# Moving a small PSUM copy from ScalarE to VectorE in a float32 Fourier transform and two-layer perceptron

## The chip, the cores and the metric

The kernel runs on one core of one Trainium2 chip. The metric is device time in microseconds, as the median of several runs. The kernel before takes 1793.97 us (median of 3 runs, 1788.93 to 1805.12).

Five engines run beside each other, each with its own queue of instructions that it works off in order: TensorE (PE in the profile; its weight loads are PEld), VectorE (DVE), ScalarE (ACT), GpSimd (POOL) and SyncE (SP, which here only issues transfers). They tell each other by semaphores what is done.

## The reference

For each of 8 batches of 3008 x 256 float32 numbers, the real part of the two-dimensional discrete Fourier transform is taken. Each of the 24064 rows of the result then goes through a perceptron with a squared ReLU:

```python
def _attn_ref(x) -> np.ndarray:
    X = np.fft.fft(x, axis=1)
    X = np.fft.fft(X, axis=2)
    return X.real.astype(np.float32)
...
def _moe_ref(x, w_in, w_out, s, b) -> np.ndarray:
    h = x @ w_in
    r = np.maximum(h, 0.0)
    g = s * (r * r) + b
    return (g @ w_out).astype(np.float32)
```

The weights are 256 x 2048 and 2048 x 256.

## The kernel before

**Transform along the sequence.** The symmetry of a real transform folds each batch into eighths on VectorE (`load`, lines 488 to 493). `transform(su, ph)` then makes the spectrum of batch `su` in two phases, `ph` 0 and 1. Each phase has four *pairs*. For a pair, TensorE makes eight small float32 matmuls of 96 columns (line 555) into one PSUM tile `ab` that holds two halves, `l[:, :, 0]` and `l[:, :, 1]`. `both` (lines 560 and 561) then takes the sum and the difference of the halves on VectorE, one half from PSUM and the other from an SBUF tile `t`. The helper `two` fills that `t`: it copies the second half out of PSUM (line 566). In phase 0 two of the four pairs call `two`, in phase 1 all four: 6 copies of 128 x 192 numbers in a batch, 48 in all. Further calls of `both` combine these into `x` and `o`, the spectrum in float32.

**Split into two reduced numbers.** `store` splits `o` into a high and a low float32r part: ScalarE casts it to `spec_h` (line 540), GpSimd subtracts to get `spec_l` (line 542).

**The perceptron.** The transform along the features is folded into the first weights at the start, so each of 3 blocks of a batch is 16 steps of `first_layer` and `second_layer`, 384 steps in all. A step's first layer is six matmuls of 502 columns into a PSUM tile `ab` (line 618), three additions on VectorE that make `h` (lines 620 to 622; the last one frees the PSUM tile), ReLU and square on ScalarE (623, 624), ScalarE's cast to `gh` (631) and GpSimd's subtraction to `gl` (634). The second layer is twelve matmuls of 502 columns into four accumulators `po` (line 651), which `finish` reads on VectorE at the end of a block (line 674).

**Buffers.** The PSUM tile `ab` has two buffers, used in turn by the pairs and by the first layers. So TensorE can start the next pair or first layer only when VectorE has read the last but one. `t` has two buffers, `x`, `o` and `lf` have one, `h`, `gh` and `gl` three.

**What sets the order.** Two strings of letters, `START` and `BATCH`, are the order in which the pieces of work are issued, and `_in_order` fixes this order on TensorE, VectorE, ScalarE and GpSimd. `L` is a first layer, `S` a second layer, `l` a piece of the next batch's folding, and `v` and `o` are pieces of the next batch's transform, phase 0 and 1. `START` holds the decoding of the weights, the transform of the first batch (`s`, `u`), all of the second's, and 57 first layers; `BATCH` is then issued in a loop, a *round* for each further batch: 48 first layers and 48 second layers of one batch with the transform of the next one between them. Six rounds have a transform in them. When a round begins, three first layers are ahead of their second layers.

The piece of code of a pair up to its `yield` issues the matmuls; what follows, the copy and the sums, comes with the next letter. In ScalarE's queue the copy stands behind the activations and casts of the first layers that were issued before it, and in VectorE's queue line 560 stands behind those layers' additions.

## Time and profile before

| | |
|---|---|
| runs | 1793.97 us, median of 3 (1788.93 to 1805.12) |
| profiled execution, its own time | 1792.28 us |
| its span, first to last instruction | 1790.2 us |
| TensorE busy | 1697.7 us, 95% |
| VectorE busy | 1281.8 us, 72% |
| ScalarE busy | 1258.8 us, 70% |
| GpSimd busy | 927.2 us, 52% |
| mean granted TensorE clock | 0.987 |
| copies of line 566 on ScalarE | 48, 14.4 us |

The start lasts until about 330 us, the six rounds with a transform from there to 1624 us, and the rest to 1790 us is the last batch's perceptron with no transform beside it. In a row of the timeline stand the start, the length, the engine, the line, the operation, output <- inputs with their shapes, how many, and in brackets how long the engine was idle before and for whom. A row of the waits has the engine with line, whom it waited for, microseconds in total, times, and the longest. Matmuls are pipelined: a matmul of 502 columns shows some 390 ns, while the next one starts 0.23 us after it.

### The profile page before, as it was taken

To read this page: it belongs to the slowest core of one execution; us is meant where nothing else is said; L and a number is where in the kernel's file an instruction comes from. 1 tells how busy PE (TensorE), PEld (TensorE's weight loads), DVE (VectorE), ACT (ScalarE), POOL (GpSimd) and SP (SyncE) were. 2 spreads that over 40 slices of the span, in tenths; PEclk is the share of its full clock that TensorE was granted. 3 is DMA by queue.
4 is the path that set the end of the run, shared out by engine and by line. 5 is a ranking of instruction groups with operands and counts; after the bars stand their busy time and mean duration, and the time that the engine had idled before them with its cause. 6 is when DMAs were issued, how large, how long until landed. Compare 5 with 4: busy or idle time off the path is not lost.

```text
span 1790.2 us, 21386 instructions
## 1 busy us (share of the span) xinstructions
PE 1697.7 (95%) x7526; PEld 1388.3 (78%) x7526; DVE 1281.8 (72%) x1957; ACT 1258.8 (70%) x1349; POOL 927.2 (52%) x562
## 2 busy tenths in 40 slices
PE   4899998999999999999999999999999999999999
PEld 3678777787787787887788777888778777788887
DVE  7888866796569766697567975679667896575554
ACT  2787776577677776776767666677776777677776
POOL 4555554454455554554545445554554554555554
PEclk9999999999999999999999999999999999999999
DMA  5321101110001100020000200002000110000000
GB/s 168 88 74 52 63 10 29 39 62 29 1 30 50 50 29 7 24 75 26 29 7 33 73 24 24 24 16 82 15 24 30 29 54 29 1 29 6 24 24 24
DMA packets 25313, 67.37 MB, mean 38 GB/s; under 512 B 4915, under 2 KB 9875, under 8 KB 25206
## 3 DMA queue, kind: packets, MB, share of 16 engines
q1 hardware_dynamic: 24934, 64.83, 11.4%
q0 software_dynamic: 272, 1.18, 0.3%
q8 instruction: 59, 0.97, 0.2%
q14 instruction: 48, 0.39, 0.1%
HBM read 41.27 MB, written 24.73 MB: 37 GB/s over the span
## 4 chain that ended last, share of the span: by engine, by line
PE 69%; DVE 17%; ACT 8%; issue 4%; DMA 1%; POOL 0%; SPq 0%; DVEq 0%; ACTq 0%; POOLq 0%
PE po L651 44%; PE ab L618 22%; DVE h L620 3%; DVE h L621 3%; ACT h L624 3%; ACT h L623 3%; DVE h L622 3%; PE ab L555 2%; ACT gh L631 2%; DVE xt L488 2%; DVE cs L493 1%; PE ab L319 1%; DVE o L674 1%; DVE xt L490 1%; DVE o L560 1%
## 5 line engine op out<-in xcount | busy, mean ns | idle before, releaser
L634 POOL TENSOR_TENSOR gl<-h,gh 128x1004 fp32r<-128x1004 f32 x373 | 811.7, 2176 | 758.2 <-ACT gh L631 482.4
L623 ACT ACTIVATE h<-h 128x1004 f32<-128x1004 f32 x384 | 400.1, 1042 | 386.3 <-DVE h L622 374.9
L620 DVE SCALAR_TENSOR_TENSOR h<-ebc,wny,ab 128x502 f32<-128x502 f32 x384 | 281.2, 732 | 299.1 <-PE ab L618 286.2
L651 PE MATMUL po<-gh,wo_h 128*128 128x502 f32 (+1 forms) x1536 | 487.0, 398 | 3.0 <-DVE o L674 3.0
L651 PE MATMUL po<-gh,wo_l 128*128 128x502 f32 (+1 forms) x1536 | 479.9, 394 | 0.0
L651 PE MATMUL po<-gl,wo_h 128*128 128x502 f32 (+1 forms) x1536 | 478.9, 393 | 0.6 <-POOL gl L634 0.6
L631 ACT CAST gh<-h 128x1004 fp32r<-128x1004 f32 x384 | 397.2, 1034 | 18.5 <-PE po L651 6.4
L624 ACT ACTIVATE h<-h 128x1004 f32<-128x1004 f32 x384 | 401.1, 1044 | 12.2
L618 PE MATMUL ab<-spec_h,wd_h 128*128 128x502 f32 x768 | 307.1, 400 | 47.2 <-DVE h L622 37.7
L651 PEld LDWEIGHTS po<-gl,wo_h 128*128 128x128 f32 x1536 | 293.5, 191 | 62.9 <-POOL gl L634 2.2
L651 PEld LDWEIGHTS po<-gh,wo_l 128*128 128x128 f32 x1536 | 293.2, 191 | 62.8
L651 PEld LDWEIGHTS po<-gh,wo_h 128*128 128x128 f32 x1536 | 290.3, 191 | 62.1 <-ACT gh L631 3.5
L618 PE MATMUL ab<-spec_l,wd_h 128*128 128x502 f32 x768 | 301.6, 393 | 0.3 <-POOL spec_l L542 0.3
L618 PE MATMUL ab<-spec_h,wd_l 128*128 128x502 f32 x768 | 300.5, 391 | 0.0
L622 DVE TENSOR_TENSOR h<-h,ab 128x502 f32<-128x502 f32 x384 | 260.4, 678 | 13.2
L621 DVE TENSOR_TENSOR h<-h,ab 128x502 f32<-128x502 f32 x384 | 260.2, 678 | 13.2
L618 PEld LDWEIGHTS ab<-spec_h,wd_h 128*128 128x128 f32 x768 | 146.6, 191 | 94.8 <-DVE h L622 52.9
L618 PEld LDWEIGHTS ab<-spec_h,wd_l 128*128 128x128 f32 x768 | 145.8, 190 | 29.4
L618 PEld LDWEIGHTS ab<-spec_l,wd_h 128*128 128x128 f32 x768 | 146.8, 191 | 27.5 <-POOL spec_l L542 0.6
L560 DVE TENSOR_TENSOR t<-ab,t 128x192 f32<-128x192 f32 x48 | 17.1, 356 | 139.6 <-ACT t L566 139.4
L542 POOL TENSOR_TENSOR spec_l<-o,spec_h 128x368 fp32r<-128x368 f32 (+3 forms) x80 | 62.0, 796 | 51.4 <-ACT spec_h L540 50.8
L540 ACT CAST spec_h<-o 128x368 fp32r<-128x368 f32 (+3 forms) x80 | 31.5, 441 | 70.9 <-DVE o L561 70.6
(91 smaller groups left out, 810.7 us busy)
## 6 DMA issues: line engine op xcount, KB each, us to landing
xt<-in_xq SPq DMA_DIRECT2D x64, 384.0 KB
out<-o SPq DMA_DIRECT2D x46, 502.0 KB
raw<-in_w_in SPq DMA_DIRECT2D x8, 512.0 KB
raw<-in_w_out SPq DMA_DIRECT2D x8, 512.0 KB
ebc<-e_dram SPq DMA_DIRECT2D x16, 251.0 KB
ebc<-e_dram SPq DMA_DIRECT2D x8, 126.0 KB
out<-o SPq DMA_DIRECT2D x4, 251.0 KB
ebc<-e_dram SPq DMA_DIRECT2D x8, 125.0 KB
```

The lines of the kernel that those rows point to most:

```text
L488: add(t[:, 0::2], t[:, 0::2], t[:, 1::2])
L542: nc.gpsimd.tensor_sub(lo, src, hi.bitcast(F32))
L555: nc.tensor.matmul(ps[:, kind, i], data[i][:, at], dft_sb[:, ph, kind, leaf + i])
L618: nc.tensor.matmul(ps[:, kind], w[:, kind, fj], m[:, kind], start=i == 0, stop=i == 2)
L620: nc.vector.scalar_tensor_tensor(h[:, 0], ebc, wny[:, j:j + 1], ps[:, 0], op0=ALU.mult, op1=ALU.add)
L621: sub(h[:, 1], h[:, 0], ps[:, 1])
L622: add(h[:, 0], h[:, 0], ps[:, 1])
L623: nc.scalar.activation(h, h, AF.Relu)
L624: nc.scalar.activation(h, h, AF.Square)
L631: nc.scalar.copy(gh[:, :, :NT], h)
L634: engine.tensor_sub(gl[:, :, :NT], h, gh[:, :, :NT].bitcast(F32))
L651: nc.tensor.matmul(po[2 * pm + dh][:, :n], l[:, j, dh * P:(dh + 1) * P], r[:, pm, :n], start=start and first, stop=stop and last,)
```

## The change

The copy of a pair's second half out of PSUM is made by VectorE in place of ScalarE:

```diff
         def two(t, l):
 
             second = t[:, :, :NL]
-            nc.scalar.copy(second, l[:, :, 1])
+            nc.vector.tensor_copy(second, l[:, :, 1])
             return l[:, :, 0], second
```

The order on TensorE and GpSimd is the same in both kernels. On ScalarE 48 instructions go, on VectorE 48 come.

First, ScalarE at the first copy of a round (`t` is the copy's SBUF tile, `ab` the pair's PSUM tile; `h` and `gh` belong to first layers):

```order
 L624 ACTIVATE h<-h 128x1004 [waits Activation_49]
 L631 CAST gh<-h 128x2x502 [waits PE_49,Activation_49]
-L566 COPY t<-ab 128x2x96
 L623 ACTIVATE h<-h 128x1004 [waits DVE_49,Pool_49]
 L624 ACTIVATE h<-h 128x1004 [waits Activation_49]
```

The copy stood behind a first layer's activations and its cast; what was behind it moves up by one.

Second, VectorE at the same place of the program, the first pair of phase 0 of a round:

```order
 L621 TENSOR_TENSOR h<-h,ab 128x502 [waits DVE_49]
 L622 TENSOR_TENSOR h<-h,ab 128x502 [waits DVE_49]
-L560 TENSOR_TENSOR t<-ab,t 128x2x4x24 [waits PE_49,Activation_49]
+L566 COPY t<-ab 128x2x96 [waits PE_49]
+L560 TENSOR_TENSOR t<-ab,t 128x2x4x24 [waits DVE_49]
 L561 TENSOR_TENSOR t<-ab,t 128x2x4x24
 L620 SCALAR_TENSOR_TENSOR h<-ebc,wny,ab 128x502 [waits PE_49,Pool_49]
```

The copy stands directly ahead of the sum that reads it, and the wait for ScalarE is replaced by one for the pair's matmuls.

Third, VectorE at the last pair of phase 0 of a round (`o` is the finished spectrum that `store` splits, `lf` the input of phase 1):

```order
 L622 TENSOR_TENSOR h<-h,ab 128x502 [waits DVE_49]
-L560 TENSOR_TENSOR t<-ab,t 128x2x96 [waits Activation_49]
-L561 TENSOR_TENSOR t<-ab,t 128x2x96
-L560 TENSOR_TENSOR o<-x,t 128x4x96 [waits DVE_49,Pool_49]
+L566 COPY t<-ab 128x2x96
+L560 TENSOR_TENSOR t<-ab,t 128x2x96 [waits DVE_49]
+L561 TENSOR_TENSOR t<-ab,t 128x2x96
+L560 TENSOR_TENSOR o<-x,t 128x4x96 [waits DVE_49,Activation_49,Pool_49]
 L561 TENSOR_TENSOR o<-x,t 128x4x96
 L349 SCALAR_TENSOR_TENSOR lf<-cs,turn_sb 96x256 x2
```

Here too the copy comes in ahead of the first sum. The sum into `o` now waits for ScalarE itself.

## The prediction

> **What bounds the kernel now.** I began with the page's span and busy shares.

> ```profile
> span 1790.2 us, 21386 instructions
> ...
> PE 1697.7 (95%) x7526; PEld 1388.3 (78%) x7526; DVE 1281.8 (72%) x1957; ACT 1258.8 (70%) x1349; POOL 927.2 (52%) x562
> ```

> TensorE is the bound. Nothing on another engine is worth time unless TensorE stands still behind it, or its clock does. So the next view was the waits, in the loop's stretch (330 to 1624 us).

> ```profile
> DVE t L560 <- ACT t L566: 117.4, 30, 4.7
> ...
> PE ab L618 <- DVE h L622: 32.1, 19, 3.4
> PE ab L555 <- DVE t L561: 13.8, 6, 2.3
> PE po L651 <- DVE o L674: 3.0, 4, 1.4
> ```

> (us in total, times, longest.) VectorE waits for 30 of the loop's 36 copies of line 566, 3.9 us on average. That is VectorE's idle time and by itself costs nothing. The other three rows are TensorE's waits in the loop, all for VectorE. The question is which of them hang on the copy. There are two such places in each of the six loop rounds.

> The first place is the first pair of a transform's first phase (rows picked from the timeline; start, length, and in brackets the idle time before):

> ```profile
> 619.17 1.03 PE L555 MATMUL ab<-dft_sb,cs 96*128 96x96 f32 x8
> 620.93 0.68 DVE L622 TENSOR_TENSOR h<-h,ab 128x502 f32<-128x502 f32 x1
> 625.51 0.31 ACT L566 COPY t<-ab 128x192 f32<-128x192 f32 x1
> 625.86 0.36 DVE L560 TENSOR_TENSOR t<-ab,t 128x192 f32<-128x192 f32 x1 [4.25 <-ACT t L566]
> 626.63 1.10 PE L555 MATMUL ab<-dft_sb,lf 96*128 96x96 f32 x8 [2.29 <-DVE t L561]
> ```

> The pair's matmuls end at 620.20 and VectorE is free at 621.61. But the copy stands in ScalarE's queue, behind the work of a first-layer step, until 625.51. VectorE cannot read the pair until 625.86, the PSUM buffer is not freed, and TensorE stands 2.29 us.

> The second place is the last pair of that phase (rows picked in the same way):

> ```profile
> 666.98 1.04 ACT L540 CAST spec_h<-o 128x380 fp32r<-128x380 f32 x2
> 671.26 2.16 POOL L634 TENSOR_TENSOR gl<-h,gh 128x1004 fp32r<-128x1004 f32 x1
> 672.21 0.68 DVE L622 TENSOR_TENSOR h<-h,ab 128x502 f32<-128x502 f32 x1
> 676.25 2.16 POOL L634 TENSOR_TENSOR gl<-h,gh 128x1004 fp32r<-128x1004 f32 x1 [2.83 <-ACT gh L631]
> 676.42 0.36 DVE L560 TENSOR_TENSOR t<-ab,t 128x192 f32<-128x192 f32 x1 [3.53 <-ACT t L566]
> 676.69 0.35 DVE L561 TENSOR_TENSOR t<-ab,t 128x192 f32<-128x192 f32 x1
> 677.14 1.68 DVE L560 TENSOR_TENSOR o<-x,t 128x384 f32<-128x384 f32 x1
> 678.42 0.38 PE L618 MATMUL ab<-spec_h,wd_l 128*128 128x502 f32 x1
> 681.47 0.68 DVE L622 TENSOR_TENSOR h<-h,ab 128x502 f32<-128x502 f32 x1
> 682.20 0.50 PE L618 MATMUL ab<-spec_h,wd_h 128*128 128x502 f32 x1 [3.40 <-DVE h L622]
> ```

> VectorE loses 3.53 us on the copy. The o of line 560 then starts beside GpSimd's line 634 and takes 1.68 us. So the h behind them is done at 682.15, and TensorE, which wants its buffer, stands 3.40 us.

> Last I looked at the clock, by stretches (us, busy PE, PEld, DVE, ACT, POOL with counts, granted clock): a round without and a round with half-rate, the six rounds together, the stretch before the loop, and three short ones of the round at 758: around its first place, and behind its second.

> ```profile
> 545.71:758.46 212.75, 205.48 (x929) 169.71 (x929) 157.17 (x239) 153.10 (x161) 112.20 (x59) 1.00 0.11 34
> 758.46:975.49 217.03, 209.87 (x930) 172.96 (x929) 157.23 (x239) 153.09 (x161) 112.29 (x59) 0.98 0.10 33
> sum 1292.84, PE 1246.45 PEld 1027.36 DVE 947.13 ACT 918.07 POOL 671.01; mean PE 207.74 PEld 171.23 DVE 157.85 ACT 153.01 POOL 111.84
> 198.00:331.48 133.48, 122.83 (x538) 100.22 (x538) 86.93 (x140) 87.68 (x97) 67.05 (x38) 0.96 0.09 27
> 837.70:841.10 3.40, 1.72 (x12) 1.64 (x13) 2.42 (x5) 0.88 (x2) 2.14 (x1) 1.00 0.01 2
> 841.10:844.50 3.40, 3.40 (x10) 2.71 (x9) 2.33 (x5) 2.39 (x3) 0.00 (x0) 0.50 0.00 0
> 895.70:902.50 6.80, 5.99 (x14) 4.81 (x15) 4.81 (x8) 5.10 (x5) 2.63 (x2) 0.50 0.00 0
> ```

> The stretch of 3.4 us in which the first place's wait leaves TensorE busy for only 1.72 us is followed by one of 3.4 us at half clock. Behind the second place it is 6.8 us. So a long wait can cost twice.

> **The change part by part.** *The copy leaves ScalarE.* 48 copies of 0.31 us leave its queue. At 70% busy it has room, so this alone is worth nothing on TensorE's path.

> *The copy joins VectorE's queue*, directly ahead of the first line 560 that reads it (the order of the instructions shows this).

> ```profile
> L566 ACT COPY t<-ab x48: 292/312/323, 19.2 to 1615.2; 128x192 f32<-128x192 f32 x48
> ...
> L560 DVE TENSOR_TENSOR t<-ab,t x48: 342/358/360, 24.9 to 1615.6; 128x192 f32<-128x192 f32 x48
> L560 DVE TENSOR_TENSOR o<-x,t x24: 557/1762/1802, 50.2 to 1616.2; 128x384 f32<-128x384 f32 x24
> ```

> (ns, shortest, median, longest.) No such copy is in the trace. Its bounds are ScalarE's 0.31 us and 0.36 us for VectorE's sum over the same PSUM half and one more operand; I take 0.35 us, nearer to the row of its own engine. What needs its result starts 0.10 us after its end, as the o above does (676.69 + 0.35, then 677.14). So a copy costs VectorE 0.45 us from its start to the start of t, 21.6 us in all. It cannot be below nothing, since an instruction is added there.

> GpSimd could make it dearer. The o sums, which read two operands from SBUF, go from 557 ns to 1802 beside GpSimd's work; the t sums, with one operand in SBUF, never leave 342 to 360. The copy reads PSUM only, so I go by the t row. If it were held up like an o, it would cost 1.2 us more, which place two below would feel as half a microsecond a round, 3 us in all. [...]

> *The wait moves from ScalarE to TensorE.* At the first place VectorE is free at 621.61 and the pair has been done since 620.20. Copy to 621.96, t from 622.06, its second sum from 622.33 to 622.68. Without the stall TensorE would ask for the buffer at 626.63 - 2.29 = 624.34, so 1.7 us of margin: the 2.29 us go.

> At the second place the copy starts at 672.89, t at 673.34, o at 674.06. GpSimd's line 634 has ended at 673.42 and its next one waits for ScalarE's cast until 676.25, so o runs in 0.56 us instead of 1.68. From o's start to the end of the last h sum it was 682.15 - 677.14 = 5.01 us; less 1.12 us that is 3.89, so 677.95. TensorE needs that buffer one matmul after 678.42, near 678.65. Margin 0.7 us: the 3.40 us go, with less to spare. One new wait appears at this o: it must now itself wait for ScalarE's casts of the o before, which the copy in ScalarE's queue had implied. They ended at 668.02, long before.

> What is queued behind the copy is the h sums of lines 620 to 622, which TensorE's buffers hang on. Where VectorE did not wait for ScalarE (6 of the loop's 36 copies, and the first batch's 6) they come up to 0.45 us later. The loop's six stand right behind another copy that did wait. The first batch's six lie in the start phase, one of them directly ahead of a wait of TensorE:

> ```profile
> 25.70 5.92 PE L451 MATMUL ab<-dft_sb,room 96*16 96x384 f32 x24 [7.73 <-DVE t L561]
> ```

> I charge half of these six, 1.3 us; bounds 0.45 and 2.7. From 198 to 330 us the second batch's transform runs inside the start, with these waits of VectorE and of TensorE:

> ```profile
> DVE t L560 <- ACT t L566: 22.0, 6, 5.1
> ```

> ```profile
> PE ab L618 <- DVE h L622: 5.3, 3, 2.7
> PE ab L618 <- DVE t L561: 5.1, 4, 2.1
> ```

> *The sum*, from the profiled execution's own 1792.3 us (its span and 2.1 us around it; 0.1% below the median of the runs):

> - first place, six rounds: 13.8 us (row of the loop's waits);
> - second place: 6 x 3.40 = 20.4 us, the six longest of the 19 waits in its 32.1 us row;
> - second batch's transform in the start: 5.3 + 5.1 = 10.4 us, where VectorE waited 22.0 us for its six copies;
> - half clock in the loop: the six rounds take 1292.84 us, six undisturbed ones 6 x 212.75 = 1276.5. Of the 16.3 us, 3.0 are the waits for line 674, which stay. 13.3 us;
> - half clock in the start: (1 - 0.96) x 133.48 = 5.3 us, less what fell into waits; I take 4.5.

> Together 62.4, less 1.3: 61.1 us. 1792.3 - 61.1 = 1731 us. What limits a round then is TensorE at full clock, 212.75 - 5.69 = 207.1 us, against 157 us of VectorE (and 2 us of copies) and 153 of ScalarE. GpSimd's gl, due next on TensorE, has cost it 0.6 us in the whole run:

> ```profile
> L651 PE MATMUL po<-gl,wo_h 128*128 128x502 f32 (+1 forms) x1536 | 478.9, 393 | 0.6 <-POOL gl L634 0.6
> ```

> **The rivals.** Early in each round, with no copy near, TensorE stands about a microsecond for a late h:

> ```profile
> 781.41 0.50 PE L618 MATMUL ab<-spec_h,wd_h 128*128 128x502 f32 x1 [1.05 <-DVE h L622]
> ```

> *The next wait stands close behind.* VectorE's freed sums run into GpSimd's line 634 elsewhere, and h is late by such a microsecond in new places. At each of the loop's 30 places where VectorE waited that is 31.5 us: 1731 + 31.5 = 1763 us. For it: the o sums are often stretched. Against: GpSimd is idle half of the time, and the long o sums came just from the copy's starting together with GpSimd, behind the same cast.

> *The short waits were not what halved the clock.* The half-rate behind the 2.29 us waits and in the start stays. The round at 758 lost 217.03 - 212.75 = 4.28 us to 10.2 us of it, of which 3.4 lie behind its first place: 1.4 us. One later round has such a stretch too: 2.9 us, and the start's 4.5. 1731 + 7.4 = 1738 us. The trace speaks against it with the 1.72 busy of 3.40 us before a half-rate stretch. [...]

> *The wait only changes its name.* The copy could wait for the pair as long as t waited for the copy: 1792 us. Both places above have the pair finished before VectorE is free, so this needs places I did not see.

> *Slower: VectorE takes the end.* If at these places what ended last were VectorE's own work and not ScalarE's queue, 48 x 0.45 = 21.6 us would come on the path: 1814 us. It decides at place two if a copy takes 0.7 us longer than I assume, so that TensorE stands again. Against it are the 117.4 us that VectorE stood idle right there.

> **How the numbers follow.** The forecast has 0.68, the close next wait 0.14, the clock 0.08, the name 0.06, slower 0.04. Low end: what is left of line 622's loop waits (32.1 - 20.4 = 11.7) and line 674's 3.0 go too: 1731.2 - 14.7 = 1716.5, less 0.8 for the start's cost at its lower bound and 0.8 for all of its 5.3 us of half clock: 1714.9, given as 1714. High end: the close next wait, 1763, and 1.4 us for the start's upper bound: 1765. One percent of the runs' median is 17.9 us, about what a measurement of this kernel can tell; faster by over that is below 1776. The forecast, the next wait and the clock lie there: 0.90; same 0.06; slower 0.04.

> **What would show it.** Right: VectorE's waits ahead of line 560 and the new copy are under 20 us in all; the 2.29 and 3.40 us waits are gone; o at place two takes near 0.56 us; the granted clock is 1.00 from 198 us on; a round takes about 207 us. Wrong: rounds near 212 us with the two waits gone (a next wait, to be named from TensorE's waits), the copy's row over 1 us, or half-rate stretches with no long wait before them.

## The result and the profile after

The kernel after takes 1706.1 us (median of 4 runs, 1705.81 to 1708.33), the one before 1796.6 us on the same chip (1788.93 to 1805.12): a ratio of 0.950 [0.945, 0.954]. The forecast was 1731, its range 1714 to 1765. The direction and the two places were right; the gain is larger than the range allowed. The profiled execution took 1708.33 us, 84.0 less than the one before.

The page of the kernel after, its span, busy shares, granted clock by slices and the chain that ended last:

```profile
span 1706.5 us, 21369 instructions
...
PE 1667.4 (98%) x7526; PEld 1379.0 (81%) x7526; DVE 1275.4 (75%) x2005; ACT 1250.6 (73%) x1301; POOL 930.0 (54%) x562
...
PEclk9999999999999999999999999999999999999999
...
PE 91%; DVE 4%; DMA 2%; ACT 2%; issue 1%; POOL 1%; SPq 0%; DVEq 0%; POOLq 0%; ACTq 0%
```

The chain of waits is now TensorE nearly throughout. Its busy time fell by 30.3 us (1697.7 to 1667.4) with the same 7526 matmuls, so some of them had run longer before; the rest of the 84 us was standing still. The waits in the loop's stretch (316 to 1540 us; us in total, times, longest), all rows in which TensorE waits for VectorE, VectorE waits at the copy, or line 674 is named:

```profile
DVE t L566 <- PE ab L555: 11.5, 12, 1.3
...
PEld ab L618 <- DVE h L622: 1.6, 1, 1.6
...
DVE o L674 <- PE po L651: 1.3, 5, 0.3
...
PE ab L618 <- DVE h L622: 1.1, 1, 1.1
```

VectorE waits 11.5 us at the copy where it had waited 117.4 at the sum. TensorE's 32.1, 13.8 and 3.0 us have become one wait of 1.1 us, in the first round. Two whole rounds by stretches (columns as in the prediction: PE, PEld, DVE, ACT, POOL, then the clock):

```profile
516.00:720.00 204.00, 204.00 (x930) 170.37 (x929) 155.60 (x245) 152.27 (x155) 112.63 (x59) 1.00 0.11 35
720.00:924.00 204.00, 204.00 (x930) 170.38 (x929) 155.58 (x245) 152.28 (x155) 112.62 (x59) 1.00 0.11 35
```

A round is 204.0 us of TensorE without a pause at full clock. The forecast had 207.1: nothing was to be left for VectorE to gain below that, and 3.1 us a round were. The copy and the long o, by their groups:

```profile
L566 DVE COPY t<-ab x48: 342/351/359, 25.0 to 1528.3; 128x192 f32<-128x192 f32 x48
...
L560 DVE TENSOR_TENSOR o<-x,t x24: 557/560/2199, 49.7 to 1529.4; 128x384 f32<-128x384 f32 x24
```

The copy takes 351 ns and no more than 359, and 347 to 352 at the 21 of the 48 places where it lies wholly beside a line 634 of GpSimd, so GpSimd did not hold it up here; the o sums' median fell from 1762 ns to 560.

The first place in the kernel after (rows picked from the timeline):

```profile
593.04 1.03 PE L555 MATMUL ab<-dft_sb,cs 96*128 96x96 f32 x8
...
594.80 0.68 DVE L622 TENSOR_TENSOR h<-h,ab 128x502 f32<-128x502 f32 x1
...
595.39 0.35 DVE L566 COPY t<-ab 128x192 f32<-128x192 f32 x1
595.78 0.36 DVE L560 TENSOR_TENSOR t<-ab,t 128x192 f32<-128x192 f32 x1
...
598.04 1.03 PE L555 MATMUL ab<-dft_sb,lf 96*128 96x96 f32 x8
```

The pair is ready at 594.07, VectorE comes to it at 595.39, and the next pair's matmuls start without a wait. The second place:

```profile
642.60 2.16 POOL L634 TENSOR_TENSOR gl<-h,gh 128x1004 fp32r<-128x1004 f32 x1
...
643.56 0.68 DVE L622 TENSOR_TENSOR h<-h,ab 128x502 f32<-128x502 f32 x1
644.15 0.35 DVE L566 COPY t<-ab 128x192 f32<-128x192 f32 x1
...
644.54 0.36 DVE L560 TENSOR_TENSOR t<-ab,t 128x192 f32<-128x192 f32 x1
...
645.29 0.56 DVE L560 TENSOR_TENSOR o<-x,t 128x384 f32<-128x384 f32 x1
...
646.24 0.87 DVE L349 SCALAR_TENSOR_TENSOR lf<-cs,turn_sb 96x256 f32<-96x256 f32 x2
...
647.59 2.16 POOL L634 TENSOR_TENSOR gl<-h,gh 128x1004 fp32r<-128x1004 f32 x1 [2.83 <-ACT gh L631]
...
648.51 0.68 DVE L622 TENSOR_TENSOR h<-h,ab 128x502 f32<-128x502 f32 x1
...
650.00 0.39 PE L618 MATMUL ab<-spec_h,wd_h 128*128 128x502 f32 x1
```

The h that TensorE needs at 650.00 is done at 649.19, a margin of 0.81 us (forecast 0.7). The t starts 0.39 us after the copy's start (forecast 0.45), and the o takes 0.56 us as forecast. All of VectorE's work of the pair, lf too, is over 0.48 us before GpSimd's line 634 starts. That gap matters in the last experiment.

**Where the 84 us came from.** I laid the two traces matmul against matmul (7526 in each) and noted by how much each one starts earlier than before:

| term | forecast, us | measured, us |
|---|---|---|
| start, to 330 us, its half clock and the copies' cost included | 13.6 | 15.8 |
| first place, six rounds | 13.8 | 15.6 |
| second place, six rounds | 20.4 | 21.8 |
| half clock in the loop | 13.3 | 12.3 |
| a short wait at a round's end (0.44 us idle), six rounds | 0 | 7.9 |
| a wait at a round's beginning (1.05 us idle), five rounds | 0 | 6.6 |
| waits for line 674, two rounds | 0 | 4.0 |
| together | 61.1 | 84.0 |

The last matmul starts 83.6 us earlier, and where one row ends and the next begins is good to some tenths of a microsecond. 18.5 of the missing 22.9 us are the last three rows.

### The profile page after: what moved, and what is told of

Its sections match the earlier page's. It is cut to its first block, busy times and chain, and to the rows that moved or that the text cites. A ratio compares the mean times of both kernels' runs of the same rounds, so it can differ in the third digit from the quotient of the medians.

```text
span 1706.5 us, 21369 instructions
## 1 busy us (share of the span) xinstructions
PE 1667.4 (98%) x7526; PEld 1379.0 (81%) x7526; DVE 1275.4 (75%) x2005; ACT 1250.6 (73%) x1301; POOL 930.0 (54%) x562
## 4 chain that ended last, share of the span: by engine, by line
PE 91%; DVE 4%; DMA 2%; ACT 2%; issue 1%; POOL 1%; SPq 0%; DVEq 0%; POOLq 0%; ACTq 0%
PE po L651 59%; PE ab L618 29%; PE ab L555 3%; DMA xt<-in_xq 1%; DVE h L620 1%; DVE h L621 1%; DVE h L622 1%; DVE xt L488 0%; ACT h L624 0%; ACT gh L631 0%; ACT h L623 0%; DMA raw<-in_w_out 0%; PE ab L451 0%; POOL gl L634 0%; DMA ebc<-e_dram 0%
## 5 line engine op out<-in xcount | busy, mean ns | idle before, releaser
L634 POOL TENSOR_TENSOR gl<-h,gh 128x1004 fp32r<-128x1004 f32 x373 | 815.5, 2186 | 707.0 <-ACT gh L631 400.1
L651 PE MATMUL po<-gh,wo_h 128*128 128x502 f32 (+1 forms) x1536 | 480.6, 394 | 0.0
L651 PE MATMUL po<-gl,wo_h 128*128 128x502 f32 (+1 forms) x1536 | 475.5, 390 | 0.6 <-POOL gl L634 0.6
L651 PE MATMUL po<-gh,wo_l 128*128 128x502 f32 (+1 forms) x1536 | 475.7, 391 | 0.0
L624 ACT ACTIVATE h<-h 128x1004 f32<-128x1004 f32 x384 | 401.2, 1045 | 12.2
L631 ACT CAST gh<-h 128x1004 fp32r<-128x1004 f32 x384 | 397.4, 1035 | 12.6 <-PE po L651 0.3
L651 PEld LDWEIGHTS po<-gl,wo_h 128*128 128x128 f32 x1536 | 290.9, 190 | 62.0 <-POOL gl L634 2.2
L651 PEld LDWEIGHTS po<-gh,wo_l 128*128 128x128 f32 x1536 | 289.9, 189 | 61.6
L651 PEld LDWEIGHTS po<-gh,wo_h 128*128 128x128 f32 x1536 | 286.3, 189 | 56.3 <-issue 0.5
L618 PE MATMUL ab<-spec_h,wd_h 128*128 128x502 f32 x768 | 301.5, 393 | 9.8 <-DVE h L622 4.9
L618 PE MATMUL ab<-spec_l,wd_h 128*128 128x502 f32 x768 | 299.5, 390 | 0.3 <-POOL spec_l L542 0.3
L618 PE MATMUL ab<-spec_h,wd_l 128*128 128x502 f32 x768 | 298.2, 388 | 0.0
L622 DVE TENSOR_TENSOR h<-h,ab 128x502 f32<-128x502 f32 x384 | 260.6, 679 | 13.3
L618 PEld LDWEIGHTS ab<-spec_h,wd_h 128*128 128x128 f32 x768 | 145.6, 190 | 43.0 <-DVE h L622 8.4
L618 PEld LDWEIGHTS ab<-spec_l,wd_h 128*128 128x128 f32 x768 | 145.7, 190 | 29.1 <-POOL spec_l L542 0.6
L618 PEld LDWEIGHTS ab<-spec_h,wd_l 128*128 128x128 f32 x768 | 144.6, 188 | 29.1
L674 DVE TENSOR_SCALAR o<-po,sb_s,bias 128x502 f32<-128x502 f32 (+1 forms) x95 | 69.3, 791 | 11.2 <-PE po L651 11.2
L488 DVE TENSOR_TENSOR xt<-xt 96x512 f32<-96x512 f32 x56 | 71.0, 1267 | 0.0
```

The lines of the kernel that those rows point to most:

```text
L488: add(t[:, 0::2], t[:, 0::2], t[:, 1::2])
L618: nc.tensor.matmul(ps[:, kind], w[:, kind, fj], m[:, kind], start=i == 0, stop=i == 2)
L622: add(h[:, 0], h[:, 0], ps[:, 1])
L624: nc.scalar.activation(h, h, AF.Square)
L631: nc.scalar.copy(gh[:, :, :NT], h)
L634: engine.tensor_sub(gl[:, :, :NT], h, gh[:, :, :NT].bitcast(F32))
```

## The experiments

Two theories of the table's last three rows were set against each other. Theory A: these waits also hang on the copy, on that of a round's last pair, which makes VectorE late. Theory B, the rival: they are collisions of VectorE and GpSimd that any shift of the round removes, so without the stalls of the first two places they go by themselves.

What the traces show, first in the kernel before (rows of PE, DVE and POOL picked; `xt` and `cs` are the folding of the next batch, whose sums read two operands in SBUF; the wait of 1.05 us at 781.41 follows and stands in the prediction):

```profile
749.73 0.36 DVE L560 TENSOR_TENSOR t<-ab,t 128x192 f32<-128x192 f32 x1 [4.74 <-ACT t L566]
...
756.84 0.50 PE L618 MATMUL ab<-spec_h,wd_h 128*128 128x502 f32 x1 [0.44 <-DVE h L622]
...
765.42 0.74 DVE L620 SCALAR_TENSOR_TENSOR h<-ebc,wny,ab 128x502 f32<-128x502 f32 x1 [1.48 <-PE ab L618]
...
767.37 2.17 POOL L634 TENSOR_TENSOR gl<-h,gh 128x1004 fp32r<-128x1004 f32 x1 [0.97 <-ACT gh L631]
...
767.50 2.58 DVE L488 TENSOR_TENSOR xt<-xt 96x512 f32<-96x512 f32 x1
...
771.00 2.37 POOL L634 TENSOR_TENSOR gl<-h,gh 128x1004 fp32r<-128x1004 f32 x1 [1.46 <-DVE xt L490]
...
771.25 2.39 DVE L493 TENSOR_TENSOR cs<-xt 96x256 f32<-96x256 f32 x1
```

and after, from the same `h` of line 620 on:

```profile
731.81 0.74 DVE L620 SCALAR_TENSOR_TENSOR h<-ebc,wny,ab 128x502 f32<-128x502 f32 x1 [2.56 <-PE ab L618]
...
733.02 2.17 POOL L634 TENSOR_TENSOR gl<-h,gh 128x1004 fp32r<-128x1004 f32 x1 [0.97 <-ACT gh L631]
...
733.89 1.83 DVE L488 TENSOR_TENSOR xt<-xt 96x512 f32<-96x512 f32 x1
...
736.90 0.41 DVE L493 TENSOR_TENSOR cs<-xt 96x256 f32<-96x256 f32 x1
...
737.39 2.16 POOL L634 TENSOR_TENSOR gl<-h,gh 128x1004 fp32r<-128x1004 f32 x1 [2.21 <-DVE cs L493]
```

At the round's end VectorE itself is late: behind the copy for which it waited 4.74 us it works without a pause, and its h comes 0.44 us too late for TensorE at 756.84.

At the next round's beginning the lateness takes another way. VectorE has caught up by 765.42: there it waits 1.48 us for TensorE. ScalarE and GpSimd, which work on the late h, have not: ScalarE has no pause from 754.81 to 767.24. So GpSimd's line 634 begins 0.13 us ahead of VectorE's line 488, which then takes 2.58 us, and 0.25 us ahead of line 493, which takes 2.39. In the kernel after, line 634 begins 0.87 us ahead of line 488 (1.83 us), and line 493 comes ahead of GpSimd and takes 0.41 us. From the end of VectorE's pause to the end of the h for which TensorE waits it is 15.94 us before and 13.34 after. The other four rounds show the same, to 0.1 us.

**Four kernels with the copy on VectorE only in part.** Phase 0 alone (two of the six copies of a batch), phase 1 alone, a batch's last pair alone, and the last pair of phase 0 alone, which is the second place:

```diff
             second = t[:, :, :NL]
-            nc.vector.tensor_copy(second, l[:, :, 1])
+            if ph == 0:            # or: ph == 1 / ph == 1 and last / ph == 0 and last
+                nc.vector.tensor_copy(second, l[:, :, 1])
+            else:
+                nc.scalar.copy(second, l[:, :, 1])
```

> Only the two copies of phase 0 go to VectorE, those at my first and second place; phase 1 keeps ScalarE's copies. Comparing TensorE's starts in the two profiles matmul by matmul, a round without half clock gains 8.8 us: 2.57 at the first place, 3.62 at the second, 1.30 at the round's end and 1.33 at its beginning, and 2.0 in two rounds at line 674. Theory A (a late VectorE): the waits at the round's end and beginning and at line 674 hang on phase 1's last copy. Then they stay here: 6 x (2.57 + 3.62) + 3.2 in the start + 13.6 of half clock = 54 us, 1738 us. Theory B (those waits are collisions of VectorE and GpSimd that any shift of the round removes): they go too, 19.6 us more, 1719 us.

> The complement: only the four copies of phase 1 go to VectorE. Theory A: the two places of phase 0 keep TensorE's waits of 2.29 and 3.40 us and the half clock behind them; the waits at the round's end and beginning and at line 674 go (19.8 us), and the start's four of phase 1 (11.5 us): 1761 us. Theory B: only the start's go, 1781 us.

> Only the last copy of phase 1 goes to VectorE (one of the six of a batch). Theory A: the waits at the round's end (1.30), at the beginning of the next (1.33) and at line 674 (2 x 2.0) go although no copy is near them, and 2.9 us of the start: 22.7 us, 1770 us. Theory B: only the start's, 1789 us.

> Only the second copy of phase 0 goes to VectorE. Both theories: TensorE's 3.40 us waits go, the 2.29 us waits stay: 6 x 3.62 + 2.5 in the start + some 10 us of half clock, 1757 us. [...]

Measured, beside 1790.7 us of the kernel before on that chip (idle of TensorE in each round, us, from the traces; "half" is the loop's time at half clock, together):

| on VectorE | first place | second place | round's end | round's beginning | half, us | time, us | ratio |
|---|---|---|---|---|---|---|---|
| none (before) | 2.30 | 3.40 | 0.44 | 1.05 to 1.09 | 30.7 | 1790.7 | |
| phase 0 | 0 | 0 | 0.46 | 1.06 to 1.11 | 0 | 1734.8 | 0.968 [0.964, 0.972] |
| phase 1 | 2.31 | 3.40 | 0 | 0 | 34.1 | 1762.1 | 0.983 [0.979, 0.987] |
| last pair | 2.31 | 3.40 | 0 | 0 | 34.1 | 1771.5 | 0.988 [0.984, 0.992] |
| second place | 2.31 | 0 | 0.45 | 1.06 to 1.09 | 10.2 | 1755.4 | 0.979 [0.974, 0.984] |

(The first round is left out of the column "round's beginning": it has a wait of 1.0 to 1.1 us there before, with phase 1 or the last pair alone and in the kernel after, and of 0.3 us with phase 0 or the second place alone.) TensorE's waits in the loop of the kernel with phase 0 alone:

```profile
PE ab L621 <- DVE h L625: 11.1, 13, 2.7
```

and one of its rounds:

```profile
555.06:761.65 206.59, 205.04 (x930) 169.94 (x928) 157.79 (x240) 152.99 (x158) 112.29 (x59) 1.00 0.11 35
```

and TensorE's waits with the last pair alone:

```profile
PE ab L621 <- DVE h L625: 21.6, 7, 3.4
...
PE ab L555 <- DVE t L561: 13.8, 6, 2.3
```

In what the two short waits hang on, theory A holds and B falls. Phase 1 alone came out at 1762.1 us (A 1761, B 1781), the last pair alone at 1771.5 (A 1770, B 1789), the second place at 1755.4 (both 1757). With both long waits gone and the last pair's copy still on ScalarE, a round is 206.6 us and the two short waits stand in every round from the second on; VectorE's pause of 1.45 to 1.48 us and the two slow folding sums (2.60 to 2.64 and 2.38 to 2.39 us) stand there too. With only the last pair's copy moved, the two long waits are all there, and the short ones are gone (7 waits, 21.6 us: six of 3.40 and the first round's); line 493 then takes 0.41 or 0.42 us. Moved alone, this copy, at which TensorE does not wait, brought 19.2 us (1790.7 - 1771.5), what it gave in the start included. B was right in one thing: at a round's beginning it is a collision that makes h late, but the last pair's copy sets it up. That the lateness gets there through ScalarE and GpSimd is read from the traces; no run holds these two back alone.

The phase 0 kernel came out 3.2 us below the 1738 that A expected. That number had left line 674's 4.0 us standing, and its trace has no wait of TensorE there. No other variant has one either. In the kernel before these waits stand where VectorE's folding runs long and line 674 comes late; which of its lateness is the copies' I have not separated.

**Is it VectorE that has to do it, or only an earlier place in a queue?** The copy stays on ScalarE, but is issued with the pair's matmuls, before the `yield`:

```diff
+            t = small.tile([P, 2, 4 * NL], F32, name="t", tag="tmp")
+            if ph == 1 or leaf in (0, 6):
+                nc.scalar.copy(t[:, :, :NL], ps[:, :, 1])
             yield
-            return small.tile([P, 2, 4 * NL], F32, name="t", tag="tmp"), ps
+            return t, ps
...
-            second = t[:, :, :NL]
-            nc.vector.tensor_copy(second, l[:, :, 1])
-            return l[:, :, 0], second
+            return l[:, :, 0], t[:, :, :NL]
```

> The copy stays on ScalarE but is issued together with the pair's matmuls, so it stands ahead of the first layers' activations that it stood behind. If the copy's place in ScalarE's queue made VectorE late, and not the engine, VectorE's waits ahead of line 560 fall to under half, most of TensorE's waits go, and ScalarE waits for the pair's matmuls instead: 1710 to 1740 us. If the hand-over between two engines is what costs, it stays near the kernel before, 1780 or more.

1751.3 us, ratio 0.972 [0.968, 0.977]: between the two. The first place in it (rows of PE, ACT and DVE picked):

```profile
606.29 1.03 PE L555 MATMUL ab<-dft_sb,cs 96*128 96x96 f32 x8
...
611.70 1.03 ACT L632 CAST gh<-h 128x1004 fp32r<-128x1004 f32 x1
612.63 0.31 ACT L558 COPY t<-ab 128x192 f32<-128x192 f32 x1
612.97 0.36 DVE L563 TENSOR_TENSOR t<-ab,t 128x192 f32<-128x192 f32 x1 [4.25 <-ACT t L558]
...
613.74 1.10 PE L555 MATMUL ab<-dft_sb,lf 96*128 96x96 f32 x8 [2.30 <-DVE t L564]
```

and the second:

```profile
658.20 0.31 ACT L558 COPY t<-ab 128x192 f32<-128x192 f32 x1
...
659.93 0.35 DVE L563 TENSOR_TENSOR t<-ab,t 128x192 f32<-128x192 f32 x1
```

At the second place a first layer lay between the matmuls and the old place of the copy. There it moved ahead, finished 1.42 us before t, and the 3.40 us are gone. At the first place nothing lay between. The pair is ready at 607.32, but ScalarE, in order, still has the activations and casts of steps whose first layers were issued before the pair, up to 612.63; the 4.25 and 2.30 us are as before. The short waits at the round's ends stay as well. Of a batch's six copies in the loop the edit changes the place of this one alone; at the other five nothing of ScalarE's stood between the pair's matmuls and the copy. So at the second place it is the place in the queue that costs, and ScalarE could make the copy there. At the first place, issued with its matmuls, the copy comes 5.3 us behind them on ScalarE, and 1.3 us behind them on VectorE in the kernel after; an order that puts it ahead of older activations on ScalarE was not tried.

**Does ScalarE's freed time count?** ScalarE makes a copy of equal size, of other data and to a spare buffer, at each of the 48 places:

```diff
             nc.vector.tensor_copy(second, l[:, :, 1])
+            nc.scalar.copy(spare, feat_sb[:, :, :NL])
```

> As the changed kernel, but ScalarE makes a copy of the same size from one SBUF table to a spare tile at the old copy's place; nobody waits for it. It gives ScalarE its 48 x 0.3 us back without VectorE's wait. If freeing ScalarE is worth nothing: 1706 us, within 2. If part of the gain comes from ScalarE's shorter queue: up to 15 us more, 1721 us.

1710.4 us (1708.59 to 1713.77), ratio 0.950 [0.946, 0.954], beside the 0.950 of the kernel after; its rounds are 204.0 us and its loop's waits are the same. The load of ScalarE is worth nothing that the runs resolve.

**What do the copies cost in the start?** Those of the first batch go back to ScalarE (`su > 0` as the condition):

```diff
-            nc.vector.tensor_copy(second, l[:, :, 1])
+            if su > 0:
+                nc.vector.tensor_copy(second, l[:, :, 1])
+            else:
+                nc.scalar.copy(second, l[:, :, 1])
```

> The first batch's six copies stay on ScalarE, all others go to VectorE. In the start VectorE hardly waited for them, and the changed kernel is 0.4 us behind the kernel before at 124 us. Expected 0.4 us less than the changed kernel: 1705.7 us. If the half-rate stretches of the start fall otherwise: up to 2 us more or less.

1707.8 us (1704.33 to 1709.79, 6 runs), ratio 0.948 [0.944, 0.951]: no difference that the runs resolve.

**How dear may the copy be?** VectorE makes each copy four, three and two times over, with the same data:

```diff
-            nc.vector.tensor_copy(second, l[:, :, 1])
+            for _ in range(4):     # or 3, 2
+                nc.vector.tensor_copy(second, l[:, :, 1])
```

> VectorE makes each copy four times in a row, 3 x 0.35 = 1.05 us more on its queue per copy, 50 us in all. In the changed kernel h at the second place is done 0.8 us before TensorE wants its buffer. Theory: what is over the margin comes on the path, 0.25 us and a refill at that place in each round, and half to all of 6 x 1.05 in the start: 1711 to 1718 us. The rival in which VectorE takes the end: all 50 us, 1756 us.

> Every copy on VectorE is made twice. At the second place the margin of 0.81 us then shrinks by 0.39 us to about 0.42, and the lf of line 349, which in the kernel after ends 0.48 us ahead of GpSimd's line 634, still ends 0.09 us ahead of it. So no wait of TensorE in the loop, and a third of the 10.5 us that three further copies cost in the start: 1709.6 us, 1707 to 1713. If instead each further copy is worth what four of them cost together, a third of 32.5 us: 1717 us, with waits in the loop.

> Every copy on VectorE is made three times. The copies alone leave a margin of 0.03 us at the second place. If only their own time counted, no wait of TensorE in the loop and two thirds of the start's 10.5 us: 1713 us. If the collision with GpSimd decides, the second lf of line 349 begins 0.14 us ahead of GpSimd's line 634 and is held up: the pair of lf takes between 1.0 and 2.8 us instead of 0.87, TensorE waits 0.1 to 1.8 us at the second place, and the time is 1714 to 1728 us. If each further copy is worth what four cost together: 1728 us.

| copies | time, us | ratio to the kernel before on the same chip | waits at the second place |
|---|---|---|---|
| 1 (after) | 1706.1 | 0.950 [0.945, 0.954] | none |
| 2 | 1709.9 | 0.948 [0.944, 0.952] | none |
| 3 | 1719.0 | 0.953 [0.949, 0.956] | one round of six, 2.12 us |
| 4 | 1738.6 | 0.965 [0.961, 0.969] | all six, 2.16 us |

Four missed both numbers: I had counted only the copies' own 1.05 us against the margin, which leaves 0.25 us of wait, and 2.16 came. Two came out as expected. Three lie in the range expected of a collision with GpSimd, though only one round of six had it; over half of the 10.5 us by which the matmuls of its trace end behind those of the kernel after was lost in the start. The second place with three copies shows why four cost so much, since it went both ways. VectorE's rows and GpSimd's next line 635 (GpSimd's `gl`, one line further down here), in one round:

```profile
649.98 1.14 DVE L567 COPY t<-ab 128x192 f32<-128x192 f32 x3
...
652.85 0.87 DVE L349 SCALAR_TENSOR_TENSOR lf<-cs,turn_sb 96x256 f32<-96x256 f32 x2
653.42 2.32 POOL L635 TENSOR_TENSOR gl<-h,gh 128x1004 fp32r<-128x1004 f32 x1 [2.83 <-ACT gh L632]
```

and in the next:

```profile
854.05 1.14 DVE L567 COPY t<-ab 128x192 f32<-128x192 f32 x3
...
857.28 2.77 DVE L349 SCALAR_TENSOR_TENSOR lf<-cs,turn_sb 96x256 f32<-96x256 f32 x2
857.51 2.27 POOL L635 TENSOR_TENSOR gl<-h,gh 128x1004 fp32r<-128x1004 f32 x1 [2.84 <-ACT gh L632]
...
862.18 0.79 PE L619 MATMUL ab<-spec_h,wd_h 128*128 128x502 f32 x1 [2.12 <-DVE h L623]
```

`lf` reads two SBUF operands there, as the o sums do. The row of lf holds two instructions. In the first round the second of them begins at 653.24, 0.18 us before GpSimd: it takes 0.47 us, VectorE goes on, and GpSimd takes 2.32 us instead of 2.16. In the other it begins at 857.68, 0.17 us after GpSimd, and takes 2.38 us; the row is 2.77 us instead of 0.87. With four copies lf is behind GpSimd in every round. So the cost of a slower copy at this place is a step: nothing in five rounds of six at 0.8 us more, and where the step comes 1.9 us at once, with a half-rate stretch behind five of these seven waits.

## Why the prediction was right or wrong

**The mechanism, at both places: right.** The 2.29 and 3.40 us waits went, the o at the second place fell to 0.56 us, VectorE's waits fell to 12.2 us at the copy and 2.2 at line 560 in the whole run (under 20 said), and the margin was 0.81 us for a forecast 0.7. That ScalarE's freed time is worth nothing was right (the load put back changed no round).

**The half clock: right, 12.3 us for 13.3.** The loop of the kernel after has none. The rival that the short waits do not halve the clock falls with the kernel that has only the second place's copy on VectorE: 2.3 us of idle at the first place, with nothing longer near. Two such waits in it, each with the stretch of 3.41 us (the raster of the last section) in which the wait lies and the next one:

```profile
405.90:409.31 3.41, 2.03 (x9) 1.34 (x8) 0.00 (x0) 3.35 (x5) 2.16 (x1) 1.00 0.00 0
409.31:412.72 3.41, 2.48 (x15) 2.27 (x16) 3.18 (x7) 0.59 (x2) 2.13 (x1) 1.00 0.00 0
617.60:621.01 3.41, 1.64 (x11) 1.57 (x12) 2.33 (x5) 0.97 (x2) 2.14 (x1) 0.99 0.00 0
621.01:624.42 3.41, 3.41 (x10) 2.67 (x9) 2.42 (x5) 2.23 (x3) 0.00 (x0) 0.51 0.00 0
```

The same wait leaves TensorE busy for 2.03 us of its stretch in one round and for 1.64 in another, and only the second is followed by half clock. Three of the six waits of that kernel were.

**The step that failed: "What limits a round then is TensorE at full clock, 212.75 - 5.69 = 207.1 us".** It subtracts the two waits at which the copy stands directly ahead, and treats every other wait of TensorE as owed to something else. The prediction quoted the wait of 1.05 us and called it one "with no copy near". Both short waits, that one and the 0.44 us at a round's end, hung on the copy of the round's last pair, for which VectorE had waited 4.74 us, the later of them 31.7 us on: 7.9 + 6.6 us, shown by the last-pair kernel. VectorE carried the lateness to the round's end. To the next round's beginning ScalarE and GpSimd carried it, past a pause of VectorE, so that VectorE's folding fell behind line 634 twice. Line 674's 3.0 us, "which stay", went too, 4.0 us as cost; for this the runs show only that it went in every variant.

**Two sizes.** The terms of the two places took TensorE's idle time. Its cost is larger: the wait of 2.29 us delayed the matmuls behind it by 2.57 us, the one of 3.40 by 3.63, and the short ones at a round's end by 1.30 us for 0.44 of idle. Behind these waits the first matmul of line 618 took 0.50 us (682.20 and 756.84 in the kernel before; 0.39 at 650.00 in the kernel after), and the pair's eight together 1.10 instead of 1.03. Over its idle time the cost is 3.2 us more at both places. The start gave 2.2 us more than said; whether its charge of 1.3 us for the first batch was due the runs do not tell, as putting those copies back gained nothing that they resolve.

**The range.** Its low end let all loop waits of lines 622 and 674 go, and still gave 1714.9, because it counted them as idle, 14.7 us, where they cost 18.5, and because it held only 1.6 us, for the start, of the two sizes above, 5.4 us. The rivals' prices lay all above the forecast. None asked what else the 117.4 us of VectorE's waits had been costing further on.

**The other rivals.** The close next wait did not come with one copy; with four it came, at the second place, where GpSimd was named as the reason. The wait did not only change its name (11.5 us for 117.4). "Slower" was to decide at a copy 0.7 us dearer; with two further copies (0.78 us) it decided in one round of six, and even four copies stay 3.5% ahead of the kernel before.

## What to carry to other kernels

When a small operation moves off an engine's queue that runs behind, look at how long its reader had waited there, and follow the lateness forward. Up to the reader's next pause, waits for it may hang on the operation. Do not stop at that pause: here the engines that the reader feeds were still late, and a collision with one of them cost time 32 us on. Put an evacuation of PSUM on the engine whose queue stands where its consumer's does, or issue it early enough on the other; idle time in all does not decide. And price a wait of a TensorE that is the bound above its idle time (here 2.57 us for 2.29), with what follows it.

## What the runs showed of the hardware

**VectorE beside GpSimd.** VectorE's second `lf`, with two operands in SBUF, took 0.47 us when it began 0.18 us ahead of GpSimd's line, and 2.38 us when it began 0.17 us behind; the folding sum of line 493 took 0.41 us ahead of line 634 (736.90 in the kernel after) and 2.39 at 771.25 in the kernel before, 0.25 us behind it. That being behind always holds a sum up is not shown: line 490 took 0.41 us at 787.86 in the kernel before, 0.01 us behind line 634, and 2.42 us at 1004.91, 0.03 us behind it. The copy out of PSUM never took more than 359 ns; the one at 644.15 us in the kernel after lies wholly beside a line 634 of GpSimd (642.60 to 644.76).
